# Two-layer attention and token-mixer kernel: the first head group's keys and queries by token tile, and three groups' weight copies on GpSimd

## The chip, the cores and the metric

The kernel runs on one core of one Trainium2 chip. A core has five instruction queues that work side by side: TensorE (PE, matmuls; its weight loads are shown apart as PEld), VectorE (DVE), ScalarE (ACT), GpSimd (POOL), and SyncE (SP), which issues most of the transfers. Each queue is worked off in order; an instruction waits for semaphores that other engines or transfers raise, and what stands behind it on its engine waits with it. The metric is the device time of one execution in microseconds (us).

## The reference

The input x has 2048 tokens of 640 features. Two layers follow each other, both with the same weights; each is an attention block and then a multi-layer perceptron that mixes tokens.

```python
x = A_x
x = x + _A_ref(_layernorm(x), A_wqkv, A_wo)                       # 32 heads of 20 features, softmax over 2048 keys
x = x + _B_ref(_layernorm(x), B_w1, B_b1, B_w2, B_b2)             # mixes tokens: 2048 -> 1536 -> 2048, gelu
x = x + _A_ref(_layernorm(x), A_wqkv, A_wo)
x = x + _B_ref(_layernorm(x), B_w1, B_b1, B_w2, B_b2)
```

In `_A_ref`, qkv is x times wqkv. Each head's scores are q·k over the square root of 20, then a softmax, then the product with v; the heads' outputs are put side by side and multiplied by wo.

## The kernel before

The 32 heads stand in eight groups of four; a group's keys and queries fill the 128 partitions (four heads of 32 rows each, 20 of them used). The queries stand in four blocks of 512, the keys in sixteen tiles of 128. A unit of work is one block, one group and one key tile; it has four chunks, one per head, of 128 keys by 512 queries. So a layer has 2048 chunks. Of most chunks ACT makes the exponential: a score tile in PSUM holds three chunks or two, in turn, so that ACT works through instructions of 1536 and 1024 columns (`emit_exp`, L781). Of 282 chunks in the first layer DVE and GpSimd make the exponential in several instructions (`ve_admit`, `ve_enqueue`, `ve_base`, `ve_shift`). `emit_S` (L717, matmuls at L711) lets PE make the scores, `emit_PV` (L1320) multiplies the exponentials by v and sums in the bank `acc`; `finish_run` (L799) takes a sum out.

The order on the engines is made when the program is built. A planner in `attention` walks through time with its own clock for PE, DVE and ACT and with costs written in the code. It emits the next score tile, the next exponential, and in between "fills" (`add_fill`, L1015; `fill_step`, L1291): small matmul groups with a due place, a readiness time, and an evacuation out of PSUM at the end. Fills are the transposes of normed tokens (`t_fill`, L1232), the value projections (`v_fill`, L1210), key and query projections (`proj_fill`, L1186), the output projection and the first mixer matmuls (`enqueue_mm1`, L1062). A fill takes one of the banks `misc` and `Dt` (`free_bank`, L1281); transposes before the first score tile may also take a score bank.

The start of the first layer is laid out by `TokenFeed.begin` (L1528). Four tiles of 128 tokens are loaded, then the raw key and query weights of the first four groups, the value weights, and two more token tiles. DVE norms a tile (bn_stats, bn_aggr, veps; GpSimd makes the reciprocal root at L911; DVE applies it at L915 and writes `h_bf`), PE transposes it, and ACT copies the transposed tile to `hT` (the buffer `hh`) at L366. `group_copy` (L1575) spreads a group's raw weights into padded ones: for groups 0 to 3 on ACT (L1582; eight copies of 400 columns), for groups 4 to 7 on DVE. When four token tiles are transposed, `t_fill`'s `after` queues the projections of groups 0 to 3 for these 512 tokens: five matmuls of 512 columns each for keys (`KT`) and queries (`QTq`). The first score tile needs both of group 0.

At the end of the layer `end_tiles` (L962) finishes the last two token tiles. Two score banks get zeros by small matmuls, ACT copies the residual x1 into them (L967), mixer fills that are still open are worked off, and then PE adds the last heads' output projection (L972). DVE takes statistics of the sums (L992), and the second layer starts from them. The mixer fills each take six matmuls of 320 columns and are added to a buffer by DVE (L1091).

Of the kernel before, what the change touches and what calls it, by code (L numbers as in the profile page):

```python
# [81 lines left out]
def kernel(  # L82
# [141 lines left out]
    def attention(st, x_in_ap, x_mid, uacc_l, feed, feed_stack):  # L224
# [299 lines left out]
        def ve_admit(t):  # L524
# [5 lines left out]
            if slot == 0:  # L530
                if len(ve_procs) > 2:
                    return
                done = backlog(now) + 2 * 1.2 + 4.0 + CFG["VE_MARGIN"]
                n = max(cursor[0] // NH + max(CFG["VE_LEAST"], math.ceil(done / 1.8)), ve_state["unit"] + 1)
                if early[0] and n >= len(units) and not far(n, now):
                    return
                if n >= NU:
                    n = max(cursor[0] // NH + math.ceil((done - CFG["VE_MARGIN"]) / 1.8), ve_state["unit"] + 1)
                if n >= NU and not early[0] and Dbank not in banks:
                    banks.append(Dbank)  # L540
                if n >= NU or not unit_ok(units[n], now - 0.1):
                    return
                ve_state["unit"] = n
# [471 lines left out]
        def add_fill(key, prio, mms, evac, w, ready=0.0, allow=None, after=None, wave=None, cells=None, cost=None,  # L1015
                     act=None, gate=None, fed=False):
# [3 lines left out]
                                   cost=cost or 0.155 + 0.00104 * w, act=act, ready=ready, allow=allow, gate=gate, fed=fed))  # L1020
# [182 lines left out]

        def enqueue_qproj(qb):
# [27 lines left out]
        def t_fill(tt, h_bf, ready, done):  # L1232
# [15 lines left out]
            def after(end):  # L1248
                tready[tt] = at = end + DVE_TO_PE
                v_fill(tt, 0, feed.wv_early, when(0, tb) + tt % 4 - 1, at, fed=True,  # L1250
                       gate=(lambda: len(tready) >= 4) if tb == 0 else None)
                if all(4 * tb + i in tready for i in range(4)):
                    for g in list(range(EG)) + rest:
                        gate = feed.gate_late if g >= EG else None
# [4 lines left out]
                        if tb == 0:  # L1259
                            proj_fill("Q", g, 0, when(g, 0) - 4, max(at, cx.w_at.get((1, g), at + 1.0)),  # L1260
                                      gate=feed.gate_late if g >= EG else None, fed=g < EG)
# [19 lines left out]
        def free_bank(now, grp):  # L1281
            use = banks + spare if grp["key"][0] == "T" and not s_start else banks
# [8 lines left out]
        def fill_step(alloc=None):  # L1291
            if fs["cur"] is None:
# [3 lines left out]
                fs.update(cur=grp, idx=0, tile=alloc() if alloc else bank.alloc(), bank=bank)  # L1296
# [6 lines left out]
            if fs["idx"] == len(grp["mms"]):  # L1303
                t, bank = fs["tile"], fs["bank"]
                fs["cur"] = None
                eng = dvm if not grp["act"] else acm if grp["key"] in feed.act_evacs else evac_engine()
# [183 lines left out]
    class TokenFeed:  # L1490
        groups = 4
        early_qbs = (0, 1)
        ve_early = True
        act_evacs = [("T", tt) for tt in range(4)]
# [33 lines left out]
        def begin(self, cx):  # L1528
# [29 lines left out]
            landing.update({4: 9.5, 5: 10.0})  # L1558
# [15 lines left out]

            def group_copy(i, g):  # L1575
                eng = cx.acm if g < self.groups else cx.dvm

                def copied(e):
                    src = raw[(i, g // 4)][:].rearrange("p a (h i) -> p a h i", i=DH)[:, :, 4 * (g % 4):4 * (g % 4) + 4, :]
                    dst = wpads[i][:, :, g, :].rearrange("p a (j i) -> p a j i", i=32)[:, :, :, 0:DH]  # L1580
                    if eng is cx.acm:
                        nc.scalar.copy(out=dst, in_=src)  # L1582
                    else:
                        nc.vector.tensor_copy(out=dst, in_=src)
# [4 lines left out]
                ready = 22.0 if g >= self.groups else 11.5 if g else (7.5, 8.7)[i]  # L1589
# [7 lines left out]
            def start_tile(tt):  # L1597
# [5 lines left out]
                def after(e):  # L1603
# [12 lines left out]
    class MixFeed:  # L1616
        groups = 4
        act_evacs = ()
# [290 lines left out]
```

## Time and profile before

| what | us |
|---|---|
| median of three runs | 1749.25 (1748.48 to 1749.32) |
| the profiled execution's own time | 1749.92 |
| its span, first to last instruction | 1747.7 |
| busy ACT, PE, DVE, POOL | 1665.2, 1674.5, 1540.8, 596.1 |
| first exponential of layer one starts | 15.44 |
| last exponential of layer one ends | 814.73 |
| first exponential of layer two starts | 851.24 |

The profiled execution is 2.2 us longer than its span, which is what lies before the first and after the last instruction. In rows of the timeline the columns are the start and the duration in us, the engine, the line, the operation, output and inputs by the program's names, the shapes, and how many equal instructions were merged; in brackets stands the idle time before it and what ended it. Records of one engine can overlap a little, since the next instruction starts while the one before drains. The granted TensorE clock was 0.999 of full speed over the run.

### The profile page before, as it was taken

To read this page: it belongs to the slowest core of one execution; us is meant where nothing else is said; L and a number is where in the kernel's file an instruction comes from. 1 tells how busy PE (TensorE), PEld (TensorE's weight loads), DVE (VectorE), ACT (ScalarE), POOL (GpSimd) and SP (SyncE) were. 2 spreads that over 40 slices of the span, in tenths; PEclk is the share of its full clock that TensorE was granted. 3 is DMA by queue.
4 is the path that set the end of the run, shared out by engine and by line. 5 is a ranking of instruction groups with operands and counts; after the bars stand their busy time and mean duration, and the time that the engine had idled before them with its cause. 6 is when DMAs were issued, how large, how long until landed. Compare 5 with 4: busy or idle time off the path is not lost.

```text
span 1747.7 us, 43017 instructions
## 1 busy us (share of the span) xinstructions
PE 1674.5 (96%) x17752; PEld 664.7 (38%) x17752; DVE 1540.8 (88%) x2511; ACT 1665.2 (95%) x1497; POOL 596.1 (34%) x951
## 2 busy tenths in 40 slices
PE   9999999999999999999999999999999999999999
PEld 3333333333333344444434433323333333444455
DVE  7789999999999999998544479999999999999973
ACT  9999999999999999999779999999999999999970
POOL 2243443443544333342000023434435443433310
PEclk9999999999999999999999999999999999999999
DMA  3020000000122010133322100001001220210245
GB/s 117 9 24 10 1 2 2 24 24 2 35 67 82 25 36 14 40 93 102 125 70 74 66 11 1 1 2 39 24 1 61 69 72 20 91 31 29 79 123 177
DMA packets 103060, 81.84 MB, mean 47 GB/s; under 512 B 51024, under 2 KB 87504, under 8 KB 102864
## 3 DMA queue, kind: packets, MB, share of 16 engines
q1 hardware_dynamic: 97328, 71.22, 13.5%
q0 software_dynamic: 5536, 7.88, 1.5%
q8 instruction: 138, 2.26, 0.5%
q14 instruction: 58, 0.48, 0.1%
HBM read 55.48 MB, written 23.59 MB: 45 GB/s over the span
## 4 chain that ended last, share of the span: by engine, by line
ACT 51%; PE 24%; issue 23%; DVE 1%; DMA 0%; SPq 0%; POOL 0%; ACTq 0%; DVEq 0%
ACT P L781 51%; PE S L711 7%; PE acc L1342 3%; PE ya L1792 2%; PE misc L1192 2%; PE acc L770 2%; PE misc L1083 2%; PE Dt L1192 1%; PE um L1779 1%; PE ya L1801 1%; PE yb L1792 1%; PE misc L1170 1%; PE misc L1216 0%; PE Dt L1216 0%; PE Dt L1711 0%
## 5 line engine op out<-in xcount | busy, mean ns | idle before, releaser
L781 ACT ACTIVATE P<-S 128x1536 bf16<-128x1536 f32 (+1 forms) x1428 | 1615.4, 1371 | 13.7 <-PE S L711 13.2
L711 PE MATMUL S<-QTq,KT 32*128 32x512 bf16 (+1 forms) x4460 | 579.0, 337 | 62.6 <-ACT P L781 45.2
L669 POOL TENSOR_SCALAR ey<-ew 128x512 f16<-128x512 uint16 x511 | 317.8, 622 | 622.4 <-DVE ey L598 257.2
L711 PEld LDWEIGHTS <-KT 32*128 32x128 bf16 x5144 | 234.7, 91 | 525.1 <-issue 495.7
L563 DVE TENSOR_SCALAR ew<-Dt 128x512 int32<-128x512 f32 x528 | 359.6, 681 | 22.5 <-PE Dt L711 14.5
L1342 PE MATMUL acc<-P,Vaug 128*32 128x512 bf16 (+1 forms) x4436 | 361.9, 343 | 0.0
L598 DVE SCALAR_TENSOR_TENSOR ey<-ey,ew 128x1024 int16<-128x1024 f16 x264 | 331.9, 1257 | 1.6
L770 PE MATMUL acc<-zr,zw 128*32 128x512 bf16 x4104 | 318.7, 383 | 1.2 <-POOL zr L155 1.2
L652 POOL TENSOR_SCALAR Pd<-ew 128x512 int16<-128x512 int16 x337 | 208.1, 620 | 226.9 <-DVE ey L598 74.7
L711 PE MATMUL Dt<-QTq,KT 32*128 32x512 bf16 (+1 forms) x684 | 203.0, 333 | 0.0
L593 DVE TENSOR_TENSOR ey<-ey 128x1024 f16<-128x1024 f16 x264 | 190.8, 723 | 1.5 <-POOL ey L669 0.3
L1342 PEld LDWEIGHTS <-Vaug 128*32 128x32 bf16 x5120 | 101.8, 94 | 172.1 <-issue 160.6
L770 PEld LDWEIGHTS <-zw 128*32 128x32 bf16 x4320 | 109.1, 96 | 92.4 <-issue 48.0
L616 DVE TENSOR_TENSOR Pd<-Pd,ey 128x1024 int16<-128x1024 int16 (+1 forms) x196 | 126.0, 643 | 6.4 <-POOL Pd L652 4.8
L618 DVE SCALAR_TENSOR_TENSOR Pd<-ew,ey 128x1024 int16<-128x1024 int16 (+1 forms) x123 | 122.5, 996 | 0.0
L911 POOL TENSOR_TENSOR rstd<-veps,mhalf 128x1 f32<-128x1 f32 x60 | 44.9, 749 | 217.2 <-DVE veps L909 195.0
L1342 PE MATMUL acc<-Pd,Vaug 128*32 128x512 bf16 (+1 forms) x684 | 103.7, 336 | 0.3 <-DVE Pd L616 0.2
L1192 PE MATMUL misc<-hh,wq_pad 128*128 128x512 bf16 x285 | 82.6, 383 | 0.6 <-DVE veps L909 0.6
L1192 PE MATMUL misc<-hh,wk_pad 128*128 128x512 bf16 x270 | 78.1, 383 | 0.0
L1083 PEld LDWEIGHTS <-w1st 128*128 128x128 bf16 x672 | 52.4, 97 | 58.0 <-issue 45.5
L1132 PE MATMUL misc<-wo_pad,attnT 128*128 128x320 bf16 x384 | 72.8, 302 | 0.0
L1083 PE MATMUL misc<-x1last,w1st 128*128 128x320 bf16 x384 | 71.4, 302 | 0.0
(144 smaller groups left out, 1189.0 us busy)
## 6 DMA issues: line engine op xcount, KB each, us to landing
w2s<-in_B_w_dram SPq DMA_DIRECT2D x16, 768.0 KB
uacc<-ustg POOLq DMA_DIRECT2D x24, 320.0 KB, 2.5
x1in<-xd SPq DMA_DIRECT2D x24, 320.0 KB
w1st<-in_B_w_dram SPq DMA_DIRECT2D x24, 256.0 KB
xd<-x2s SPq DMA_DIRECT2D x16, 320.0 KB
xin<-xd SPq DMA_DIRECT2D x16, 320.0 KB
w1st<-in_B_w_dram SPq DMA_DIRECT2D x21, 192.0 KB
xd<-x1s SPq DMA_DIRECT2D x12, 320.0 KB
```

The costliest lines, as they stand in the source:

```text
L563: nc.vector.tensor_scalar(out=w[:, slot, :], in0=Dt[:, :], scalar1=127.0 * FIX, scalar2=0.0, op0=ALU.add, op1=ALU.max)
L593: nc.vector.tensor_tensor(out=y, in0=y, in1=y, op=ALU.mult)
L598: nc.vector.scalar_tensor_tensor(out=box["t"][:, 0:512 * k], in0=y[:, 0:512 * k], scalar=MANT_C * MANT_K ** 2, in1=frac, op0=ALU.add, op1= ...
L616: nc.vector.tensor_tensor(out=bits, in0=bits, in1=t, op=ALU.add)
L652: after_vector(nc.gpsimd.tensor_scalar(out=bits, in0=whole, scalar1=128.0, scalar2=0.0, op0=ALU.mult, op1=ALU.add))
L669: return engine.tensor_scalar(out=out_ap, in0=in_ap, scalar1=MANT_K / FIX, scalar2=-MANT_K * MANT_S, op0=ALU.mult, op1=ALU.add)
L711: pe(nc.tensor.matmul(out_ap[:, c0:c0 + w], lhsT=KT[32 * j:32 * j + 32, g, kt * 128:(kt + 1) * 128], rhs=get_QT(st, qb)[32 * j:32 * j + 32 ...
L770: pe(nc.tensor.matmul(bank[32 * j:32 * j + 32, 0:w], lhsT=zw[:], rhs=zr[:, :, 0:64].to_broadcast([128, w // 64, 64]), start=start, stop=st ...
L781: nc.scalar.activation(out=P[:, 0:ncs, :].rearrange("p a b -> p (a b)"), in_=St[:, 0:ncs, :].rearrange("p a b -> p (a b)"), func=ACT.Exp, ...
L1083: pe(nc.tensor.matmul(t[:, 0:w], lhsT=w1_of[(p, ft)][:, sti, :], rhs=rows_in[sti][:, c0:c1], start=(sti == 0), stop=(sti == n_in - 1)))
L1192: pe(nc.tensor.matmul(t[:, :], lhsT=wpad[:, dt_, g, :], rhs=hT[:, dt_, tb * 512:(tb + 1) * 512], start=(dt_ == 0), stop=(dt_ == NDT - 1)))
L1342: pe(nc.tensor.matmul(acc[32 * j:32 * j + 32, a0:a0 + w], lhsT=Vaug[:, (kt * H + hh_) * VW:(kt * H + hh_) * VW + 32], rhs=P[:, slot, c0:c0 ...
```

## The change

Four things change in the code; the first layer alone has `piecewise` set.

- Group 0's keys and queries for the first 512 tokens are no longer two fills of five matmuls with 512 columns. `proj_piece` queues, for each of the four token tiles as soon as it is transposed, five matmuls of 128 columns for keys and five for queries, into a quarter of a bank that is held for them (`own`): `Dt` for keys, the two-chunk score tile (`spare[0]`) for queries. Only the fourth piece has an evacuation: keys by the evacuation rule, queries by ACT.
- Weights of groups 1 to 3 are no longer copied by ACT but by GpSimd (`pool_copies`): group 1 after ACT's copy of group 0's query weights, groups 2 and 3 after the sixth token tile is normed. A projection fill of these groups is now held back until its weights have a time (`gate`).
- The planner's landing times of token tiles 4 and 5 are 0.5 us later.
- In `ve_admit` (both layers) the second half of a DVE pair picks a new unit where its unit has been passed.

In the order of the built program, PE, ACT, DVE and GpSimd have the same instructions in the same order from the end of the first layer (the ACT copies at L967 and the DVE statistics at L992) to the end. Up to there the planner's order changes in many places. Both programs have 282 DVE chunks and 707 ACT exponentials in the first layer: 353 of 1536 columns, 353 of 1024 and one of 512 before; 352 of 1536 and 355 of 1024 after.

```diff
@@ ve_admit
-            if slot == 0:
-                if len(ve_procs) > 2:
+            if slot == 0 or ve_state["unit"] <= cursor[0] // NH:
+                if slot == 0 and len(ve_procs) > 2:
                     return
...
+        def proj_piece(i, tt, ready):
+            wpad, bank = (wk_pad, wq_pad)[i], (Dbank, spare[0])[i]
+            if tt == 0:
+                bank.held, bank.free = bank.alloc(), 1e9
+            mms = []
+            for dt_ in range(NDT):
+                def mm(t, dt_=dt_):
+                    pe(nc.tensor.matmul(t[:, tt * 128:(tt + 1) * 128], lhsT=wpad[:, dt_, 0, :],
+                                        rhs=hT[:, dt_, tt * 128:(tt + 1) * 128], start=(dt_ == 0), stop=(dt_ == NDT - 1)))
+                mms.append(mm)
+
+            def evac(t, end, eng):
+                copy_on(eng, (get_QT(st, 0) if i else KT)[:, 0, 0:512], t[:, :], q_scale if i else None)
+
+            def after(end):
+                kready[("Q", 0, 0) if i else ("K", 0, 0)] = end + DVE_TO_PE
+            add_fill(("piece", i), -5.0 + 0.01 * tt, mms, evac if tt == 3 else None, 512, ready=ready, after=after, act=0.6,
+                     wave=0.0575, cells=0.25, gate=lambda: (i, 0) in cx.w_at, fed=tt == 3, own=bank)
...
+                pieces_first = feed.piecewise and tb == 0
+                if pieces_first:
+                    for i in range(2):
+                        proj_piece(i, tt, at)
                 if all(4 * tb + i in tready for i in range(4)):
-                    for g in list(range(EG)) + rest:
-                        gate = feed.gate_late if g >= EG else None
+                    for g in list(range(int(pieces_first), EG)) + rest:
+                        gate = feed.gate_late if g >= EG else lambda g=g: (0, g) in cx.w_at
...
         def free_bank(now, grp):
+            if grp["own"] is not None:
+                return grp["own"]
...
-        act_evacs = [("T", tt) for tt in range(4)]
+        act_evacs = [("T", tt) for tt in range(4)] + [("piece", 1)]
...
-            landing.update({4: 9.5, 5: 10.0})
+            landing.update({4: 10.0, 5: 10.5})
...
+            def pool_copies(e, gs):
+                for n, (g, i) in enumerate((g, i) for g in gs for i in range(2)):
+                    nc.gpsimd.tensor_copy(out=wpad_view(i, g), in_=raw_view(i, g))
+                    cx.w_at[(i, g)] = e + 1.0 + 0.7 * n
...
                 def done(e):
                     cx.w_at[(i, g)] = e + 0.05
+                    if (i, g) == (1, 0):
+                        pool_copies(e, (1,))
...
             for g in range(NG):
                 for i in range(2):
-                    group_copy(i, g)
+                    if g == 0 or g >= self.groups:
+                        group_copy(i, g)
...
                     if tt == 5:
                         load_rest()
+                        pool_copies(e, (2, 3))
```

More of the change, by code (lines that the diff above doesn't have):

```diff
@@ L1019, in add_fill @@
                                    wave=wave or (WAVE if w > 320 else HALF), cells=cells or w / 512,
-                                   cost=cost or 0.155 + 0.00104 * w, act=act, ready=ready, allow=allow, gate=gate, fed=fed))
+                                   cost=cost or 0.155 + 0.00104 * w, act=act, ready=ready, allow=allow, gate=gate, fed=fed, own=own))
             fill_queue.sort(key=lambda f: f["prio"])
@@ L1295, in fill_step @@
                 bank = None if alloc else free_bank(pem["t"], grp)
-                fs.update(cur=grp, idx=0, tile=alloc() if alloc else bank.alloc(), bank=bank)
+                fs.update(cur=grp, idx=0, tile=alloc() if alloc else bank.alloc() if grp["own"] is None else bank.held, bank=bank)
                 if bank:
@@ L1617 @@
         groups = 4
+        piecewise = False
         act_evacs = ()
```

20 lines of the change are left out of this document (11 added, 9 removed).

## The prediction

> **What bounds the kernel now.** I read the page's groups first, then what ACT waits for, then the timeline of the stretches that the change touches: the start and the end of the first layer.
>
> ```profile
> PE 1674.5 (96%) x17752; PEld 664.7 (38%) x17752; DVE 1540.8 (88%) x2511; ACT 1665.2 (95%) x1497; POOL 596.1 (34%) x951
> L781 ACT ACTIVATE P<-S 128x1536 bf16<-128x1536 f32 (+1 forms) x1428 | 1615.4, 1371 | 13.7 <-PE S L711 13.2
> ...
> ACT P L781 <- PE S L711: 2.7, 2, 2.3
> ```
>
> The exponentials take 1615 of 1748 us, and up to 862 us ACT waited for scores only twice, 2.3 us of it before the very first one. From there to the end of layer one ACT bounds: a start earlier by t brings the end of the exponentials earlier by t, if none waits on the way. PE is as busy, but fills its gaps with zero matmuls. Now the start:
>
> ```profile
> 8.07 0.54 ACT L1582 COPY wk_pad<-w_raw 128x400 bf16<-128x400 bf16 x1
> 9.09 0.55 ACT L1582 COPY wq_pad<-w_raw 128x400 bf16<-128x400 bf16 x1
> 9.88 0.69 ACT L366 COPY hh<-Dt 128x640 bf16<-128x640 bf16 x1 [0.25 <-PE Dt L1240]
> 15.44 1.45 ACT L781 ACTIVATE P<-S 128x1536 bf16<-128x1536 f32 x1 [2.32 <-PE S L711]
> ...
> 9.39 0.45 PE L1240 MATMUL Dt<-ident,h_bf 128*128 128x128 bf16 x5
> 9.69 0.84 PE L1216 MATMUL misc<-x1last,hh 128*128 128x320 bf16 x5
> 10.63 1.24 PE L1192 MATMUL Dt<-hh,wk_pad 128*128 128x512 bf16 x5
> 12.46 1.24 PE L1192 MATMUL misc<-hh,wq_pad 128*128 128x512 bf16 x5 [0.59 <-DVE veps L909]
> ...
> 11.96 0.45 DVE L370 CAST Vaug<-misc 128x320 bf16<-128x320 f32 x1
> 13.49 0.69 DVE L370 CAST KT<-Dt 128x512 bf16<-128x512 f32 x1
> 14.10 0.68 DVE L372 TENSOR_SCALAR QTq<-misc 128x512 bf16<-128x512 f32 x1
> ```
>
> Keys are projected by 11.87 but leave PSUM only at 13.49, since DVE norms tiles 4 and 5 first; the queries wait for a bank and follow at 14.10; a value fill follows, and the first exponential starts at 15.44. The end of layer one:
>
> ```profile
> 799.46 15.27 ACT L781 ACTIVATE P<-S 128x1024 bf16<-128x1024 f32 x14
> ...
> 815.04 0.73 PE L770 MATMUL S<-zr,zw 128*32 128x512 bf16 x16
> 815.70 0.44 PE L1083 MATMUL misc<-hh,w1st 128*128 128x320 bf16 x2
> 816.33 1.53 PE L972 MATMUL S<-wo_pad,attnT 128*128 128x512 bf16 x8 [0.18 <-ACT S L967]
> ...
> 815.29 0.45 DVE L818 STREAM_TRANSPOSE T<-acc 128x256 f32<-128x256 f32 x1 [0.64 <-PE acc L1342]
> 816.37 0.45 DVE L842 STREAM_TRANSPOSE attnT<-T 128x256 bf16<-128x256 bf16 x1
> 816.74 0.45 DVE L1091 TENSOR_TENSOR KT<-misc,KT 128x320 f32<-128x320 f32 x1
> 817.43 0.90 DVE L992 BATCH_NORM_STATS2 bnst<-S 128x6 f32<-128x320 f32 x2 [0.23 <-PE S L972]
> ```
>
> The last exponential ends at 814.73 (call it E). The statistics that open layer two start at 817.43, E+2.70. Everything behind them is the same program in the same order, so only three terms count: when the exponentials start, whether one waits, and the distance from E to the statistics.
>
> **Term 1, the start.** Up to the third tile's transpose PE and ACT run as before. Key pieces of tiles 0 and 1 start when ACT's key weights are copied (8.07+0.54) and are done before the query weights end at 9.09+0.55 = 9.64. The first query piece waits for those, and in the changed order the fourth tile's transpose stands behind it on PE. A piece is five matmuls of 128 columns, as a transpose is: 0.30 (9.39 to 9.69). So query piece 9.68 to 9.97, transpose to 10.27, ACT's copy 0.49 after the transpose's start (9.39 to 9.88), 10.46 to 11.15. Three more pieces fit in between. The last two, 11.20 to 11.49 and to 11.79, come from the fourth tile. ACT evacuates the queries at 11.49+0.49 = 11.98. No row has this copy: a cast of 320 columns on ACT took 0.43, a copy of 640 0.70; I take 0.64, the mean of the two exponentials of 512 columns, done at 12.62. DVE's key copy stands behind the norm of tile 5; without the value cast at 11.96 it starts at 12.02 and ends at 12.71 (0.69). PE does one value fill to 12.45 and two matmuls of the next, which wait for the key copy: 12.76 to 13.03. The scores then start at 13.05; from scores to exponential it was 15.01 to 15.44, 0.43. First exponential: 13.48, 1.96 earlier. Bounds: a piece cannot beat 0.30 by any row; were it half of a 512-column fill (0.54), the two last pieces add 0.5 and those before them up to 0.7, so the start lies between 13.4 and 14.7. ACT loses six copies that ended at 13.13, while it waited anyway: nothing.
>
> **Term 2, waits on the way.** Six GpSimd copies of 400 columns are new. The nearest GpSimd row is 0.62 for 512 two-byte columns (L669), the T2 memset of 512 was 0.52; I take 0.62, bounds 0.4 and 1.3 (two passes). The queue runs rstd of tile 3 (ends 8.86), two copies to 10.10, rstd of tiles 4 and 5 (11.93, to 13.10 as now), four copies to 15.6, rstd of tile 6, which DVE wants at about 19.7 (its apply was at 20.42). Cover: 1.8 us at the first pair, 4 at the second; gone at 8.86+6d+1.65 = 19.7, d = 1.5 per copy, and from there each 0.1 costs up to 0.6. PE wants group 1's weights near 13.9, group 2's near 21: nothing. The x loads of tiles 10 and 11 on SP wait for DVE's apply of tiles 4 and 5, now behind the key copy, 0.3 later; the raw weights behind them are read at 28.4: nothing. A short score tile (two chunks for three) appears at the thirteenth exponential, where group 2's queries are just in time; exponentials keep one price per chunk and one per instruction, and both totals are unchanged (353+353+1 against 352+355): nothing. The copies were not tied to a DVE instruction, as GpSimd's other copies are. DVE's L598 took 1.65 at 796.21 instead of 1.21 while a GpSimd operation ran: 0.44. The apply of tile 3 (8.89) meets the first copy; 0.44, even 0.62, ends it by 9.96, and the transpose behind it waits for the query piece until 9.97. Hidden; if both copies hold it (1.24), 0.63 is paid.
>
> The Trainium skill, "SBUF — State Buffer", section "Who interferes with whom", speaks against the change here: GpSimd and a DVE instruction in a two-port mode exclude each other for a whole instruction. An apply of 0.43 at 5.77 inside an rstd of 0.70 shows no such block, though that operand is one column; by the rule the apply of tile 3 would wait for one copy, which is covered, or for two, the 0.63 above.
>
> Elsewhere in the layer 353 pairs take 799.29 us, 2.26 each; the first fifteen exponentials run at the same rate, so the body gives nothing back and I allow 1 us either way for its new order.
>
> **Term 3, the end.** Before, two mixer matmuls are left between the zeros and the output projection. After, ten: four that finish a fill in `misc`, and six of the next fill, in the same bank. These six wait until DVE has emptied the first, and that copy stands on DVE behind the transposes of the last heads. On PE the output projection stands behind the six. Counted from E: the last score tile waits for the exponential that ends at E-1.85 (two narrow ones of 0.91 follow it: a pair takes 2.26, a wide one 1.35); then 0.33 scores, one and six and two mixer matmuls of 0.14 (0.84 for five with their drain, 0.14 apart), and 24 PV matmuls instead of 16 with the last 8 behind E: the last PV starts near E+0.43 (now E+0.23). DVE's transpose E+0.77 (now E+0.57), attnT 1.08 later, E+1.85, the copy of `misc` 0.37 later, E+2.22 to E+2.67. Six matmuls: E+2.72 to E+3.56. Of the eight projection matmuls the statistics need four. Now they follow attnT's end (816.82) by 0.61 with two of these to do; with all four, a 512- and a 128-column one more (0.22 and 0.06), less the 0.05 of the wait: 0.83, so E+4.39. Now E+2.70: 1.68 lost. Bounds: 0.9, if the fill starts with the zeros done and PE alone counts (eight more matmuls at 0.14, less 0.2 of wait now), and 2.1 if DVE's last pair is late by 0.4.
>
> **Sum.** -1.96 + 0 + 1.68 = -0.28 us on the profiled execution, 1749.92 to 1749.64. The runs shown have their median 0.67 below it; on 1749.25 it makes 1749.0.
>
> **Rivals.** (a) The end costs nothing, because the six matmuls find their bank empty: 1749.25-1.96 = 1747.3. For it: DVE had 2.09 and 0.64 us of idle time just there. Against: in the order built, the copy that empties the bank stands behind attnT. (b) The start's gain is smaller (apply held by both GpSimd copies, or slow pieces): 13.48+0.63 to 14.7, that is 1749.6 to 1750.2. (c) Slower: GpSimd's copies take over 2.2 us each, whether strided reads or the shared port make them so. Then rstd of tile 6 is late, with it DVE's queue and group 2's queries, and ACT waits at the fourteenth exponential: 8.86+15.0+1.65-19.7 = 5.8 at d = 2.5, 1754.8. It passes 0.2% from d = 2.2, 3.5 times the row. (d) The new order of the body happens to save over 1.5 us and the end costs nothing: below 1745.7; only sizes of single stalls speak for it.
>
> **How the numbers follow.** 0.2%, about what a measurement of this kernel can tell from no change, is 3.5 us: 1745.75 to 1752.75. The forecast as summed 0.55, (a) 0.15, (b) 0.15, (c) 0.09, (d) 0.06. Forecast, (a) and (b) lie within 0.2%: 0.85; faster 0.06; slower 0.09. The range for 8 in 10 takes the bounds of terms 1 and 3 and 1 us of the body: from 1747.1 (gain 2.0, loss 0.9, body -1) to 1751.2 (gain 0.8, loss 1.8, body +1).
>
> **What would show it.** First exponential near 13.5; GpSimd copies of 0.6; no wait of ACT for scores between there and E, with E near 812.8; at the end six w1st matmuls that start after the attnT transpose, and the statistics 4.4 us behind E instead of 2.7; from there the old times less 0.3. Wrong would make it: GpSimd copies over 1.5 us, an ACT wait near 28 us, the apply of tile 3 ending past 10, or the six matmuls starting before attnT.

## The result, and the profile after

The changed kernel took 1756.17 us (median of six runs, 1754.90 to 1756.45) against 1749.24 us of the kernel before on the same chip (six runs, 1748.48 to 1750.85). The ratio is 1.0037 with a 95% interval of 1.0026 to 1.0048: slower by 7 us, outside the range of 1747.1 to 1751.2.

From the page of the changed kernel, the granted clock in 40 slices and its first group:

```profile
PEclk9998999999999999999999999999999999999999
L781 ACT ACTIVATE P<-S 128x1536 bf16<-128x1536 f32 (+1 forms) x1428 | 1615.8, 1362 | 18.0 <-PE S L711 16.2
```

The exponentials take as long as before (1615.8 against 1615.4 us), but ACT stands idle for 18.0 us ahead of them and not 13.7, mostly waiting for scores, and the fourth slice (132 to 175 us) shows a clock of 0.8. The spans of the two profiled executions (1747.71 and 1754.40 us) can be cut into five pieces that add up:

| stretch | before | after | difference |
|---|---|---|---|
| to the first exponential | 15.44 | 14.11 | -1.33 |
| first to last exponential of layer one (term 2's body) | 799.28 | 806.60 | +7.32 |
| last exponential to layer two's first | 36.51 | 38.18 | +1.67 |
| layer two's exponentials | 827.03 | 826.07 | -0.96 |
| the rest | 69.45 | 69.44 | -0.01 |

So the loss is in the stretch for which the prediction wrote zero. What ACT waits for from the first exponential to the end of layer one, in the changed kernel (us in total, times, longest):

```profile
ACT P L781 <- PE S L711: 5.9, 4, 4.4
ACT P L781 <- PE Dt L711: 1.1, 1, 1.1
```

Of the first row 0.7 us lie ahead of the first exponential. Nearly all of the rest lies in one place. The next view cuts the time into windows of 5 us (busy time of PE, PEld, DVE, ACT and POOL, the granted clock, DMA share, GB/s):

```profile
130.00:135.00 5.00, 4.31 (x36) 1.81 (x35) 2.27 (x4) 5.00 (x5) 4.90 (x5) 1.00 0.61 31
135.00:140.00 5.00, 1.66 (x8) 0.68 (x8) 3.49 (x6) 1.47 (x2) 2.62 (x4) 0.61 0.96 75
140.00:145.00 5.00, 4.67 (x31) 0.91 (x28) 3.88 (x9) 3.01 (x3) 2.29 (x4) 0.50 0.28 65
145.00:150.00 5.00, 5.00 (x40) 1.52 (x40) 3.46 (x7) 4.60 (x5) 1.88 (x4) 0.87 0.00 0
```

ACT is full until 135 us and then has 1.47 and 3.01 of 5 us. One window earlier DVE falls to 2.27 while POOL is full with 4.90. The timeline of POOL, DVE, PE and ACT there, engine by engine:

```profile
127.18 4.37 POOL L1550 MEMSET wo_pad<- 128x5120 bf16 x1
131.49 1.25 POOL L183 DMA_DIRECT2D b_t<-in_B_b_dram  x1
132.75 1.16 POOL L184 DMA_DIRECT2D b_t<-in_B_b_dram  x1
133.93 0.64 POOL L652 TENSOR_SCALAR Pd<-ew 128x512 int16<-128x512 int16 x1
134.65 0.62 POOL L669 TENSOR_SCALAR ey<-ew 128x512 f16<-128x512 uint16 x1
135.34 0.62 POOL L652 TENSOR_SCALAR Pd<-ew 128x512 int16<-128x512 int16 x1
...
126.22 0.65 DVE L370 CAST KT<-misc 128x512 bf16<-128x512 f32 x1
...
131.59 0.68 DVE L563 TENSOR_SCALAR ew<-Dt 128x512 int32<-128x512 f32 x1
136.00 0.69 DVE L616 TENSOR_TENSOR Pd<-Pd,ey 128x1024 int16<-128x1024 int16 x1 [3.73 <-POOL Pd L652]
137.20 0.69 DVE L593 TENSOR_TENSOR ey<-ey 128x1024 f16<-128x1024 f16 x1 [0.51 <-POOL ey L669]
137.81 0.48 DVE L370 CAST Vaug<-misc 128x320 bf16<-128x320 f32 x1
...
134.26 0.39 PE L711 MATMUL S<-QTq,KT 32*128 32x512 bf16 x2
138.34 1.49 PE L1235 MATMUL misc<-x1last,hh 128*128 128x320 bf16 x5 [3.70 <-DVE Vaug L370]
...
140.90 2.36 ACT L781 ACTIVATE P<-S 128x1536 bf16<-128x1536 f32 x2 [4.43 <-PE S L711]
144.36 2.53 ACT L781 ACTIVATE P<-S 128x1536 bf16<-128x1536 f32 x2 [1.10 <-PE Dt L711]
```

Read it from the last row back. ACT waits 4.43 us for scores. PE can't make them: in its queue a value fill stands ahead, and that waits 3.70 us for its bank, which DVE has to empty (the `Vaug` cast at 137.81). DVE's cast stands behind an addition (L616) that waits 3.73 us for a piece of `Pd` from POOL, the one that ends at 135.96. POOL is late with it because it was zeroing `wo_pad` for 4.37 us and then issued two bias loads (1.25 and 1.16 us), 6.8 us in one block; the first piece behind the block starts only at 133.93. The diff doesn't touch these three instructions. They are issued in `after_end`, and the planner's clock of GpSimd (`port`) leaves them out. `after_end` is called as soon as all fills of the token feed are done: transposes, the first values, the keys and queries of groups 0 to 3. The last of the weight copies, at 33.5 us, is long done by then; the fill that comes last is a projection of keys, whose cast ends at 126.87. Behind the wait the granted clock is 0.50 for 10 us, which costs ACT more.

The same block in the kernel before, where nobody waits for it:

```profile
118.52 0.68 DVE L370 CAST KT<-misc 128x512 bf16<-128x512 f32 x1
...
119.36 4.37 POOL L1522 MEMSET wo_pad<- 128x5120 bf16 x1
...
126.09 1.22 POOL L652 TENSOR_SCALAR Pd<-ew 128x512 int16<-128x512 int16 x2
...
129.58 0.68 DVE L616 TENSOR_TENSOR Pd<-Pd,ey 128x1024 int16<-128x1024 int16 x1
```

DVE wanted the two pieces only at 129.58; they were ready at 127.31. The change moved the last key cast, and with it the block, by nearly 8 us (from 119.4 to 127.2), and the chunks of DVE about it. Which of the change's edits made that cast later no run separates.

Set each pitch of the exponentials (the distance of an end from the end before) against what is usual (1.344 us for 1536 columns, 0.9165 for 1024): between 135 and 148 us of the changed kernel the excess is 4.53, 1.21, 0.16 and 0.45, together 6.35 of the 7.32 us. Most of the 0.97 left are small waits too: 0.54 at 43.6 us for keys and four of 0.13 to 0.25, where the kernel before has three of 0.12 to 0.20.

The start in the changed kernel, the rows that answer to those of the prediction (ACT, then DVE, then PE):

```profile
11.33 0.69 ACT L366 COPY hh<-misc 128x640 bf16<-128x640 bf16 x1 [0.82 <-PE misc L1259]
12.83 0.60 ACT L368 ACTIVATE QTq<-S 128x512 bf16<-128x512 f32 x1 [0.81 <-PE S L1211]
14.11 1.45 ACT L781 ACTIVATE P<-S 128x1536 bf16<-128x1536 f32 x1 [0.69 <-PE S L711]
...
10.14 0.49 DVE L894 BATCH_NORM_STATS2 bnst<-x0in 128x6 f32<-128x320 bf16 x1 [0.68 <-DMA x0in<-in_A_x_dram]
12.55 0.69 DVE L370 CAST KT<-Dt 128x512 bf16<-128x512 f32 x1 [0.23 <-PE Dt L1211]
...
3.69 3.66 PE L770 MATMUL acc<-zr,zw 128*32 128x512 bf16 x40
```

ACT's copy of the fourth tile and the queries' evacuation are some 0.85 us later than forecast, the keys' cast 0.53 and the first exponential 0.63. The lateness is there from the first transposes on: the forty zero matmuls ahead of them took 3.66 us, where they took 2.79 before. The GpSimd copies took 0.51 to 0.62 us each, as taken.

The end of layer one, PE then DVE; the last exponential ended at 820.71:

```profile
823.45 0.97 PE L1083 MATMUL misc<-hh,w1st 128*128 128x320 bf16 x6 [0.83 <-DVE KT L1091]
824.26 1.25 PE L972 MATMUL S<-wo_pad,attnT 128*128 128x512 bf16 x7
...
825.08 0.90 DVE L992 BATCH_NORM_STATS2 bnst<-S 128x6 f32<-128x320 f32 x2
```

The statistics start 4.37 us behind the last exponential, against 2.70 before, with the six mixer matmuls behind DVE's copy, as the prediction had it (4.39).

### The profile page after: what moved, and what is told of

It is laid out like the page before. It is cut to its first block, busy times and chain, and to the rows that moved or that the text cites. A ratio compares the mean times of both kernels' runs of the same rounds, so it can differ in the third digit from the quotient of the medians.

```text
span 1754.4 us, 42991 instructions
## 1 busy us (share of the span) xinstructions
PE 1666.6 (95%) x17680; PEld 664.0 (38%) x17760; DVE 1541.2 (88%) x2520; ACT 1663.7 (95%) x1492; POOL 602.0 (34%) x961
## 4 chain that ended last, share of the span: by engine, by line
ACT 50%; PE 26%; issue 22%; DVE 1%; POOL 1%; another core or an unknown queue 0%; ACTq 0%; DVEq 0%; POOLq 0%
ACT P L781 49%; PE S L711 8%; PE acc L1369 4%; PE acc L770 2%; PE misc L1083 2%; PE ya L1831 2%; PE misc L1192 2%; PE um L1818 1%; PE misc L1170 1%; PE ya L1840 1%; PE yb L1831 1%; PE Dt L1750 0%; PE Dt L711 0%; PE misc L1132 0%; PE misc L1750 0%
## 5 line engine op out<-in xcount | busy, mean ns | idle before, releaser
L781 ACT ACTIVATE P<-S 128x1536 bf16<-128x1536 f32 (+1 forms) x1428 | 1615.8, 1362 | 18.0 <-PE S L711 16.2
L652 POOL TENSOR_SCALAR Pd<-ew 128x512 int16<-128x512 int16 x342 | 211.8, 621 | 237.9 <-DVE ey L598 79.7
L616 DVE TENSOR_TENSOR Pd<-Pd,ey 128x1024 int16<-128x1024 int16 (+1 forms) x202 | 127.4, 631 | 9.8 <-POOL Pd L652 8.0
L618 DVE SCALAR_TENSOR_TENSOR Pd<-ew,ey 128x512 int16<-128x512 int16 (+1 forms) x124 | 120.1, 969 | 0.0
L1192 PE MATMUL misc<-hh,wq_pad 128*128 128x512 bf16 x247 | 75.8, 386 | 2.6 <-issue 1.8
L1192 PE MATMUL misc<-hh,wk_pad 128*128 128x512 bf16 x242 | 74.2, 383 | 1.6 <-issue 1.1
```

What stands on the lines that cost most here:

```text
L616: nc.vector.tensor_tensor(out=bits, in0=bits, in1=t, op=ALU.add)
L652: after_vector(nc.gpsimd.tensor_scalar(out=bits, in0=whole, scalar1=128.0, scalar2=0.0, op0=ALU.mult, op1=ALU.add))
L781: nc.scalar.activation(out=P[:, 0:ncs, :].rearrange("p a b -> p (a b)"), in_=St[:, 0:ncs, :].rearrange("p a b -> p (a b)"), func=ACT.Exp, ...
L1192: pe(nc.tensor.matmul(t[:, :], lhsT=wpad[:, dt_, g, :], rhs=hT[:, dt_, tb * 512:(tb + 1) * 512], start=(dt_ == 0), stop=(dt_ == NDT - 1)))
```

## The experiments

The theory from the trace: GpSimd's unplanned block of 6.8 us meets a piece that DVE needs at once, and from there the wait runs through DVE's and PE's queues to ACT; then the clock drops. The rivals: the new order starves ACT anyway; the clock falls by itself; the projections by token tile are at fault.

**Zeroing early.** Only the three GpSimd instructions move, to a stretch where POOL stood idle; the planner calls `wo_early` at each of its steps.

```diff
+        def wo_early(self, now):
+            if now > 103.3 and not self.wo_done:
+                self.wo_done = True
+                nc.gpsimd.memset(wo_pad[:], 0.0)
+                setup_biases()
...
         def after_end(self, cx):
-            nc.gpsimd.memset(wo_pad[:], 0.0)
             setup_wo()
-            setup_biases()
```

> The changed kernel with one thing moved: GpSimd's zeroing of wo_pad (4.37 us) and its two bias loads (1.25 and 1.16 us) are issued at the plan's 103.3 us, where GpSimd stood idle from 104.5 to 115.2 us, and not behind the last weight copy near 127 us. Every other instruction keeps its place. Theory (the loss in layer one is GpSimd's 6.8 us block standing ahead of the Pd piece that VectorE waits 3.73 us for): the stretched pitches of the exponential between 135 and 148 us (6.35 us together) go, so 1756.2 - 6.35 = 1749.8 us; VectorE waits for GpSimd's Pd near 132 us under 0.5 us, and the granted clock there stays 1.00. Rival (the new order of the tiles, with one exponential more of the narrow form, starves ScalarE whatever GpSimd does, or the clock falls by itself): 1756 us and the 0.5 clock at 140 to 145 us again.

Measured: 1750.02 us (before 1749.09; ratio 1.0006, 0.9997 to 1.0015). The stretch of exponentials took 800.26 us and not 806.60, and ACT's waits in it came down to one row; the clock was 1.00 in all four windows from 130 to 150 us:

```profile
ACT P L781 <- PE S L711: 1.7, 2, 1.3
```

```profile
135.00:140.00 5.00, 4.67 (x42) 1.76 (x42) 4.97 (x9) 5.00 (x5) 1.93 (x4) 1.00 0.00 0
```

All of the 6.35 us went with the place of three instructions that the change does not touch. (What the expectation calls the last weight copy near 127 us is the cast of the last projected keys.) (Of the 1.7 us, 1.3 lie ahead of the first exponential.)

**Only the bias loads early.** The same hook with `setup_biases()` alone.

> The changed kernel with only the two bias loads moved to GpSimd's idle stretch; the zeroing of 4.37 us stays near 127 us. GpSimd then comes free about 2.4 us sooner, so that VectorE's wait for Pd is 3.73 - 2.4 = 1.3 us. If the loss goes with the length of that wait (linear): a third of 6.35 us stays, 2.2 us, and the kernel takes 1752.0 us. If a short wait is covered by the score tile that already lies ready and only a long one lets the clock fall: 0 to 0.8 us stays, 1749.8 to 1750.6 us. If GpSimd isn't the cause: 1756 us.

Measured: 1752.96 us (ratio 1.0021, 1.0012 to 1.0030), 0.96 over the expected 1752.0; in the profile (1752.24) 2.21 us of excess stay, 1.10 at 137.6 and 1.11 at 141.0. DVE's wait is 1.3 us as worked out. In the profile the loss is a third, as the linear theory had it, but it lies in two pitches, one behind the wait and one while the clock is low again (a row of PE's timeline, then a window); how much of it the clock makes was not tried here:

```profile
136.06 0.84 PE L1235 MATMUL misc<-x1last,hh 128*128 128x320 bf16 x5 [1.26 <-DVE Vaug L370]
```

```profile
135.00:140.00 5.00, 3.94 (x31) 1.16 (x30) 5.00 (x9) 3.98 (x4) 1.85 (x3) 0.72 0.31 71
```

**Zeroing late, in the kernel before.** Without any part of the change, `after_end`'s three pieces are issued by such a hook at the first step behind the plan's 132.3 us.

```diff
         def after_end(self, cx):
-            nc.gpsimd.memset(wo_pad[:], 0.0)
-            setup_wo()
-            setup_biases()
+            self.wo_due = True
```

> The kernel before with the same three pieces (zeroing of wo_pad, its 32 loads, the two bias loads) issued some 14 us later, at the plan's 132.3 us, where GpSimd has an ey piece or Pd piece to deliver every 2 us. Nothing of the change is in it. Theory (what costs is where the 6.8 us block meets the pieces, not the token tiles' projections): VectorE waits 3 to 5 us for GpSimd's ey or Pd near 137 to 142 us, ScalarE starves behind it, and the kernel before becomes slower by 3 to 7 us: 1752 to 1756 us. Rival (the block is harmless in the order of before, and it is the new order that has no room): 1749.2 us, within 1 us.

Measured: 1753.68 us (ratio 1.0026, 1.0017 to 1.0035). The same kind of chain, made in the kernel before; here DVE waits for `ey`, and PE for DVE's transpose that empties the bank of the sums:

```profile
132.42 4.36 POOL L1527 MEMSET wo_pad<- 128x5120 bf16 x1
...
140.56 0.69 DVE L593 TENSOR_TENSOR ey<-ey 128x1024 f16<-128x1024 f16 x1 [3.06 <-POOL ey L669]
...
143.48 0.62 PE L1342 MATMUL acc<-P,Vaug 128*32 128x512 bf16 x4 [2.65 <-DVE T L818]
...
145.17 1.02 ACT L781 ACTIVATE P<-S 128x1024 bf16<-128x1024 f32 x1 [2.52 <-PE S L711]
```

The excess there is 2.63, 1.07, 0.18 and 0.52, together 4.40 us, and the stretch took 803.68 us (799.28 + 4.40). The granted clock fell here too, to 0.50 from 142.4 to 149.2 us. The order of before is not immune; it was only luckier.

**The stall filled.** The block stays; sixteen waves of zero matmuls keep PE busy while it waits.

```diff
                 def mm(t, dt_=dt_):
+                    if layer == 0 and part == 1 and dt_ == 0 and tt == 3:
+                        acc = runs[pv_run[0]]["acc"]
+                        for _ in range(16):
+                            for j in range(4):
+                                pe(nc.tensor.matmul(acc[32 * j:32 * j + 32, 0:512], lhsT=zw[:], rhs=zr[:, :, 0:64].to_broadcast([128, 8, 64]),
+                                                    start=False, stop=False, skip_group_check=True, tile_position=(0, 32 * j)))
```

> The changed kernel, with GpSimd's block where it was, and sixteen waves of zero matmuls (some 0.21 us each, 3.4 us together) added to the running accumulator right ahead of the value matmul that stood 3.7 us waiting at 134.6 us. They need nothing that is late and end before that wait does, so the wait for VectorE and GpSimd is the same and only TensorE doesn't stand idle. Theory (of the 6.35 us, 4.53 are the wait itself and 1.82 us the three stretched exponentials behind it, run at half clock): the granted clock stays 1.00 from 135 to 150 us, the first stretched pitch is 4.3 to 4.6 us too long and the next three no more than 0.3 us together: 1754.4 to 1754.8 us. Rival (the second loss comes from VectorE's and GpSimd's work being late, not from the clock): 1.8 us behind the wait again, 1756.2 us.

Measured: 1753.60 us (ratio 1.0027, 1.0016 to 1.0038). DVE's wait is the same 3.73 us, the clock stays at 1.00, and only one pitch is too long, by 3.45 us:

```profile
133.96 3.64 PE L1239 MATMUL acc<-zr,zw 128*32 128x512 bf16 x64
...
135.37 0.69 DVE L616 TENSOR_TENSOR Pd<-Pd,ey 128x1024 int16<-128x1024 int16 x1 [3.73 <-POOL Pd L652]
```

```profile
135.00:140.00 5.00, 4.87 (x72) 2.08 (x67) 4.12 (x7) 1.66 (x2) 2.60 (x4) 1.00 0.56 83
```

So of 6.35 us the wait is 3.45 and the clock 2.90: more than the 1.82 expected, since the first matmuls behind the wait run at full speed too and ACT restarts 1.08 us sooner.

**The block counted.** One line teaches the planner what GpSimd does (`port`, the planner's clock of GpSimd, is handed to `cx` for it).

```diff
             setup_wo()
             setup_biases()
+            cx.port["t"] = max(cx.port["t"], cx.pem["t"]) + 6.8
```

> The changed kernel with one line more: where the zeroing and the bias loads are issued, the planner's clock of GpSimd is moved on by 6.8 us, which it had left out. The block stays where it is; the pieces that the plan gave GpSimd behind it go to VectorE or later. Theory (a planner that didn't count the block is what made VectorE wait): no wait of VectorE for GpSimd above 1 us near 127 to 140 us, the stretch of exponentials 800.3 us within 0.7, and 1749.5 to 1750.5 us at an end of layer one as in the changed kernel. Rival (VectorE, which has to do the pieces itself, is late by as much): a stall of 2 us or more remains, 1752 us or above.

Measured: 1748.99 us (ratio 0.9999, 0.9990 to 1.0007). The block is where it was (127.38), but DVE does the pieces itself there, in two-slot instructions, and waits 0.3 us at most for POOL; the stretch took 800.17 us:

```profile
131.17 1.22 DVE L618 SCALAR_TENSOR_TENSOR Pd<-ew,ey 128x1024 int16<-128x1024 int16 x1
...
133.30 1.33 DVE L669 TENSOR_SCALAR ey<-ew 128x1024 f16<-128x1024 uint16 x1
```

That is the repair of the cause: not another place, but a true cost.

**The end, in two steps.** With the zeroing early, the left-over fill takes the bank `Dt`; in a second kernel (zeroing cut into eight pieces, one every 4 us of the plan, then the bias loads) the fill follows the out-projection. The `tail_banks` lines below are the first kernel's edit, the others the second's; the zeroing early of the first is as above.

```diff
+            while self.wo_n < NG + 2 and now > 60.0 + 4.0 * self.wo_n:
+                n, self.wo_n = self.wo_n, self.wo_n + 1
+                if n < NG:
+                    nc.gpsimd.memset(wo_pad[:, n, :], 0.0)
+                else:
+                    setup_biases(n - NG)
...
-        tail_banks = [misc.alloc, Dbank.alloc, lambda: sums[0][:, 1024:1536]]
+        tail_banks = [(misc, Dbank)[1 - layer].alloc, (misc, Dbank)[layer].alloc, lambda: sums[0][:, 1024:1536]]
...
-        room = pem["t"] + 1.3
+        room = pem["t"] + (1.3 if layer else 0.0)
```

> As the run with zeroing and biases early, and at the end of layer one the first fill that is left over takes the other bank of PSUM (Dt) and not misc, whose evacuation it had to wait for. Prediction's term 3 (six mixer matmuls wait for VectorE's evacuation, +1.68 us): VectorE's first statistics come 2.70 us behind the last exponential and not 4.38, and the kernel is 1.68 us faster than its pair: 1748.1 us, some 1.1 us under the kernel before. Rival (another wait takes its place at once): 1749.8 us and statistics at 4.4 us.

> The changed kernel with the zeroing of wo_pad cut into eight pieces of 0.55 us, one every 4 us of the plan from 60 us on, then the two bias loads one by one; and at the end of layer one the left-over second fill (six mixer matmuls, 6 x 0.14 us) is issued behind the last out-projection matmuls and not ahead of them. The run with the other bank took 0.99 of the 1.68 us away (statistics at +3.38); theory: the remaining 0.69 us are the six matmuls themselves, so the statistics come at +2.70 us as in the kernel before and layer two's first exponential 36.5 us behind the last of layer one; the kernel takes 1748.3 us (1750.0 with zeroing early, less 1.67). Rival (the fill is only moved and delays layer two's entrance by the same amount): statistics at +2.70, but layer two's first exponential still at 37.2 to 38.2.

Measured: 1748.67 us (ratio 0.9997, 0.9989 to 1.0006) and 1748.19 us (0.9994, 0.9985 to 1.0003). The statistics start 3.38 and 2.93 us behind the last exponential, layer two's first exponential 37.19 and 36.74 us (38.18 in the changed kernel, 36.51 before). The first, then the second:

```profile
815.91 0.98 PE L1083 MATMUL Dt<-hh,w1st 128*128 128x320 bf16 x6
816.73 1.25 PE L972 MATMUL S<-wo_pad,attnT 128*128 128x512 bf16 x7
```

```profile
816.23 0.76 PE L974 MATMUL S<-wo_pad,attnT 128*128 128x128 bf16 x5 [0.34 <-DVE attnT L844]
816.82 0.98 PE L1085 MATMUL misc<-hh,w1st 128*128 128x320 bf16 x6
```

Both were expected at +2.70. Of the 1.67 us the bank was 0.99 and the six matmuls' own time on PE 0.45. The 0.23 that stay lie in front of the out-projection: DVE's transpose of the last heads starts 0.79 us behind the last exponential (814.41 in the second run, 821.50 in the changed kernel) and 0.56 before (815.29). The fill behind the out-projection delays nothing that layer two waits for.

**The admission rule taken back**, with the spread zeroing.

```diff
-            if slot == 0 or ve_state["unit"] <= cursor[0] // NH:
-                if slot == 0 and len(ve_procs) > 2:
+            if slot == 0:
+                if len(ve_procs) > 2:
```

> The changed kernel with the spread zeroing and with VectorE's admission rule (the first hunk of the change) taken back. With the block out of the way the exponential stretch of layer one still takes 800.26 us against 799.28 before. Theory: the admission rule makes that 0.98 us, and without it the stretch takes 799.3 us (0.3 either way), the kernel 1749.0 us. Rival (it comes from the start: with scores 1.3 us earlier the exponential meets keys and queries that aren't yet there, 0.54 us of it at 43 us): 800.3 us and 1750.0 us.

Measured: 1749.84 us (ratio 1.0004, 0.9995 to 1.0012); stretch 800.25. PE, DVE and ACT have the same instructions in the same order as in the changed kernel, so the first hunk of the change has no part in the result, and the expected 0.98 us were not its. The run also shows a start as early as the prediction had it, 13.38 us, and with it why the start differs from run to run:

```profile
9.74 0.49 DVE L896 BATCH_NORM_STATS2 bnst<-x0in 128x6 f32<-128x320 bf16 x1 [0.26 <-DMA x0in<-in_A_x_dram]
11.84 0.68 DVE L372 CAST KT<-Dt 128x512 bf16<-128x512 f32 x1
13.38 4.63 ACT L783 ACTIVATE P<-S 128x1536 bf16<-128x1536 f32 x4 [0.86 <-PE S L713]
```

The keys' cast stands on DVE behind the statistics of tile 4, and those wait for that tile's load. In the run with zeroing early the load was later by 1.11 us, and so was everything behind it:

```profile
10.85 0.49 DVE L894 BATCH_NORM_STATS2 bnst<-x0in 128x6 f32<-128x320 bf16 x1 [1.43 <-DMA x0in<-in_A_x_dram]
12.94 0.68 DVE L370 CAST KT<-Dt 128x512 bf16<-128x512 f32 x1
14.47 3.71 ACT L781 ACTIVATE P<-S 128x1536 bf16<-128x1536 f32 x3 [1.26 <-PE S L711]
```

In the nine profiles that have this start, the first exponential comes at the later of two times: 3.63 us behind the start of tile 4's statistics, or 2.09 us behind the end of ACT's copy of the fourth transposed tile. That fits all nine within 0.03 us (13.38 to 14.47). In the changed kernel's own profile it is the second (12.02 + 2.09), pushed back by the zero matmuls. In the two profiles with the order of before it is 5.39 us behind the same statistics (10.05 and 15.44; 11.30 and 16.68). Where that load sets the start, the change is worth 5.39 - 3.63 = 1.76 us.

**The two halves of the start.** Both with the spread zeroing: one kernel has no pieces but GpSimd's copies, the other has the pieces and ACT's copies.

```diff
-        piecewise = True
+        piecewise = False
```

```diff
-                    if (i, g) == (1, 0):
-                        pool_copies(e, (1,))
...
-                        pool_copies(e, (2, 3))
...
-                    if g == 0 or g >= self.groups:
-                        group_copy(i, g)
+                    group_copy(i, g)
```

> The changed kernel with the spread zeroing and without the token-tile pieces: the first head group's keys and queries are projected over four token tiles at once, as before; three groups' weights are still copied by GpSimd. Prediction's term 1 put the gain on both together. Theory A (ScalarE, free of six copies, now evacuates values and keys at once, and that alone brings most): the values' evacuation on ScalarE at 10.6 us, keys' matmuls 10.6 to 11.9, queries' 11.9 to 13.1, QTq by 13.9, first exponential 14.4 to 14.7 us against 13.9 to 14.5 with pieces. Theory B (the pieces bring it): first exponential at 15.3 to 15.5 us as before.

> The changed kernel with the spread zeroing, with the token-tile pieces but with the three groups' weights copied by ScalarE again (six copies of 0.53 us, a pitch of 0.43). Three of them fall between the last transposed tile's copy and QTq, one behind QTq, two among the first exponentials. Theory: QTq moves from 12.8 to 13.3 us, the first exponential to 14.3 to 14.8 us, and the copies behind it stretch the exponentials by 0.9 us: 1.2 to 1.7 us slower than with GpSimd's copies. Rival (VectorE's KT cast, late behind the statistics of tiles 4 and 5, sets the first exponential anyway): first exponential unchanged at 14.2, and only the 0.9 us behind it are lost.

Measured: 1750.51 us (ratio 1.0008, 0.9999 to 1.0017) and 1748.95 us (0.9999, 0.9990 to 1.0008). By the time alone, theory B would hold for whole groups (first exponential 15.58); but that run's load was late (statistics of tile 4 at 10.90), and from there it is 4.68 us: 0.71 less than before, so that in this one profile GpSimd's copies alone bring 0.71 of the 1.76 us, the pieces the rest. With ACT's copies the first exponential came at 14.30, 4.39 us behind the statistics, and two copies stretched the first pitches by 0.42 us each, as expected. But the kernel was not slower for it by 1.2 to 1.7 us; it was 0.9 faster (1748.95 against 1749.84 for the run above, which has GpSimd's copies): this plan has no wait at 43 us (0.54), and its end is the shorter one, +36.72, where the changed order has +38.18.

**The block counted and the end first**, both edits together:

> The block counted, and the end of layer one with the left-over fill behind the out-projection: both of the losses taken away by what the planner does, with the zeroing left in place. Expected: 1.4 to 1.7 us below the run with the block counted, 1747.9 to 1748.7 us, half a microsecond to one below the kernel before. Rival: the end is another one, since the plan of layer one is another one, and nothing is gained by the second edit.

Measured: 1748.54 us (ratio 0.9997, 0.9988 to 1.0006): 0.45 below its pair and not 1.4, since the counted plan already had the shorter wait at the end (+37.19).

**Keys by ScalarE.** The spread zeroing and the end first; in addition ACT evacuates group 0's keys.

```diff
-        act_evacs = [("T", tt) for tt in range(4)] + [("piece", 1)]
+        act_evacs = [("T", tt) for tt in range(4)] + [("piece", 0), ("piece", 1)]
```

> The changed kernel with the spread zeroing and the end as in the run with the end first; in addition ScalarE evacuates the first head group's keys too, so that they no longer stand on VectorE behind the statistics of token tiles 4 and 5. In the profiles so far VectorE casts the keys 2.09 to 2.10 us behind the start of tile 4's statistics, which wait for that tile's load (9.7 to 10.9 us), and the first exponential starts 3.62 to 3.65 us behind them. Theory (tile 4's load sets the start): here that tie is cut; the key copy stands on ScalarE behind the fourth transposed tile's copy, QTq 0.6 us behind it, two value fills on TensorE, and the first exponential comes 2.3 to 2.7 us behind the end of that copy, near 13.5 us with an early load as with a late one. Where tile 4's load is late (10.4 us or more) the distance from its statistics to the first exponential falls below 3.3 us. Kernel: 1747.5 to 1748.3 us. Rival (TensorE's pieces set the start anyway): the first exponential no earlier than in the runs before, 14.0 us or later with a late load, 1748.2 us.

Measured: 1747.00 us (11 runs, 1746.46 to 1747.69) against 1748.90: ratio 0.9989, 0.9980 to 0.9998, the only kernel whose interval lies below one, and 9 us under the changed kernel. Its profile doesn't show the reason that was expected: there the load was late (10.96) and the first transposes as well, since the zero matmuls ran slowly until 7.1 us; ACT's copy of the fourth tile ended only at 12.40, and the first exponential followed 2.50 us behind it, as expected, but at 14.90 and 3.94 us behind the statistics, where under 3.3 was expected. What it shows is another plan: a stretch of 799.14 us, without the wait at 43 us, and an end of +36.51 as in the kernel before. What the earlier keys are worth is open.

## Why the prediction was wrong

The forecast was 1749.0 us with 0.85 for no measurable change, and the kernel is 7 us slower. Two of three terms hold, one fell.

- **Term 1, the start: mechanism right, size off.** Forecast 13.48, shown 14.11 in the profile of the changed kernel and 13.38 in two of the nine of this order. The pieces, the transpose behind the query weights, ACT's evacuation and the scores came in the order and at the durations taken; QTq took 0.60 for the 0.64 assumed. What was left out is that two inputs of the sum are not fixed: tile 4's load (statistics from 9.7 to 10.9 us) and the time at which TensorE gets its full clock (6.3 us in the profile of the changed kernel, 4.5 in that of before). The gain of 1.96 is 1.76 where the load sets the start, and was 1.33 in the profiled pair; the bounds of 13.4 to 14.7 held in the nine profiles, but for 0.02 us (13.38 to 14.47).
- **Term 2, waits on the way: this step failed.** "The body gives nothing back and I allow 1 us either way for its new order" was argued from rates. It cost 7.32 us, 6.35 of them by one block on GpSimd. The prediction counted what the change adds to POOL's queue (six copies, rightly sized: 0.51 to 0.62 us, rstd of tile 6 at 19.51, on time), but not what it moves in it: `after_end` follows the last fill of the token feed, which the change made later, and 4.37 us of zeroing stood in the trace of before at 119.36, longer than any other POOL instruction. The planner doesn't count it, so it planned pieces for GpSimd right behind it. The zeroing early, the zeroing late in the kernel before, and the block counted show the cause from three sides.
- **Rival (c)** had the right engine and the right chain, GpSimd late, DVE's queue behind it, ACT without scores, with the wrong instruction and place: copies of over 2.2 us at 20 us. It gave 1754.8; that this is near the measured 1756.17 is luck, since the copies took what the forecast took and that wait never came.
- **The new tile order, 0.97 us** of the body, is within the 1 us allowed. The narrow score tile cost nothing; the admission rule changes no instruction.
- **Term 3, the end: right.** Statistics 4.37 us behind the last exponential, forecast 4.39; six matmuls behind DVE's copy of `misc`. The shares that the runs show are 0.99 for the bank, 0.45 for the matmuls themselves, and 0.23 for the later last transposes, for which the prediction had 0.20 (E+0.77 for E+0.57).
- **The upper end of the range**, 1751.2, takes a loss of 1.8 us at the end, where term 3's own bound is 2.1. With that it would be near 1751.5, still far below what was measured.
- **The apply of tile 3** took 0.61 us beside GpSimd's copies (0.45 before) and ended at 9.46, before the 9.97 that would have mattered. By "SBUF — State Buffer" in the Trainium skill, "Who interferes with whom", it would have waited until the copy that was under way had ended (8.77 to 9.28), 0.43 from its start at 8.85; the trace shows it 0.16 longer.
- **Layer two, -0.96 us** in the profiled pair, is no effect of the change: the profiled execution of before ran at half clock from 885.2 to 888.6 us, and the same program in the run with zeroing late took 825.82 us there and not 827.03.

## What to carry to other kernels

When a change moves an emission point, list everything that is issued at that point, on every queue, and look for long instructions there that nobody is waiting for yet; an engine that is busy a third of the time can still hold the bounding one if 6.8 us of it come in one piece. A planner that leaves an instruction out of its cost can put needed work behind it: giving the block its true cost (one line) brought the stretch of exponentials down as far as moving it did (800.17 and 800.26 us). And before a gain of a microsecond is summed from one profile, see which of its inputs (a load's landing, the clock's rise) differ from run to run.

## What the runs showed of the hardware

The clock drop costs nearly as much as the wait that causes it (2.90 against 3.45 us). That sixteen waves of zeros took the drop away shows that idling caused it in the changed kernel. How much idling it takes the runs don't settle. From the windows of 1 us: in the changed kernel PE stood idle from 134.65 us; the granted clock fell to 0.50 at 136.1 and came back at 146.3. With the zeroing late in the kernel before, PE stood idle from 140.83 to 143.48, and the clock was 0.50 from 142.4 to 149.2. In the run with the bias loads early an idle time of 1.26 us (134.80 to 136.06) was followed by 0.50 from 137.2 to 140.6. In the kernel before gaps of 0.48, 0.19 and 0.19 us within 882.0 to 884.8 were followed by 0.50 from 885.2 to 888.6. But the run with the block counted has the same three gaps in the same place (882.4 to 885.2), and the run with whole groups an idle time of 1.23 us (358.67 to 359.90), and in both the clock stayed at 1.00. So what made the clock fall at 885.2 is open.

The half clock lasted 10.2, 6.8, 3.4 and 3.4 us. "TensorE: Matmul & The Clock Gate" in the Trainium skill, Part 1, has a free-running activity window of about 3.4 us, and these lengths agree with it: three windows, two, one and one. Its later section "Why this matters for your kernels" asks only that gaps stay under about 3 us; here the clock fell behind a single gap of 1.26 us and once with none over 0.48, so the measurement decides: to stay under 3 us was not enough.

At the start the zero matmuls ran from 1.18 us on, and their duration fell from 0.63 to 0.38 us somewhere between 3.7 us (the block counted and the end first) and 7.1 us (keys by ScalarE), the instant differing from profile to profile, though the instructions are the same up to there. The spread of 3.4 us is one such window of the Trainium skill; no run here sets its phase.
